# Placing VectorE's side work between two multiply-adds, and a strip of a gate on GpSimd

## The chip, the cores and the metric

One core of a Trainium2 chip. The metric is device time in microseconds (us), the median of the fast runs; executions of one kernel agree within about 0.2%. Five engines work side by side, each on its own list of instructions in order: TensorE (matrix products; PE, and PEld for its weight loads), VectorE (DVE), ScalarE (ACT), GpSimd (POOL) and SyncE (SP, which only starts transfers). They wait for one another through semaphores.

## The reference

Two parts, one after the other, for x of 8 x 3136 x 256 in float32:

```python
X = np.fft.fft(np.fft.fft(x, axis=1), axis=2).real          # mixing
h = np.maximum(X @ w_in, 0.0)                               # 256 -> 1024
conv = sum(conv_w[k] * shifted(h, k - 1) for k in range(3)) # along the sequence, per feature
out = (h * (1 / (1 + np.exp(-conv)))) @ w_out               # 1024 -> 256
```

## The kernel before

The transform along the sequence is done with products against DFT tables, after VectorE has *folded* the input (sums and differences of mirrored rows). The results of two half transforms are joined in *DFT sums* on VectorE. The transform along features is merged into `w_in`, as the matrix G. Then come 256 steps (8 batches x 4 chunks x 8 blocks of 128 features). In cycle t of the main loop, each engine works on several steps at once:

```python
for t in range(n + LAG):                      # LAG = 3
    sigmoid(steps[t - 2])                     # ScalarE, in two parts: GpSimd's columns, then VectorE's
    run("first")
    products(steps[t + 1])                    # TensorE: pb and pa, 386 to 418 columns
    copies(steps[t + 1])                      # ScalarE: pb from PSUM to SBUF, twice
    run("act")                                # ScalarE's copy for a DFT sum (u.copy)
    combine(steps[t])                         # VectorE, two instructions: h = relu(pa +- pb)
    run("dve")                                # VectorE: a fold, a DFT sum (u.fin) or a narrowing of weights
    seed(steps[t + 2])                        # ScalarE
    first_tap(steps[t])                       # ScalarE: g = w0 * h
    other_taps(steps[t - 1])                  # VectorE: g = w1 * h' + g, then g = w2 * h'' + g
    gate(steps[t - 2])                        # g = g * h, half on GpSimd and half on VectorE
    run("load")
    mm2(steps[t - LAG])                       # TensorE: the second product, po
    run("pe")                                 # TensorE: products pd of the next batch's DFT
```

(The guards at both ends of the loop are cut.) The side work for the next batch is spread over the cycles of this one. A DFT sum adds one half that ScalarE has copied out of PSUM and one that is still there:

```python
def copy(p):
    a_[sn, c] = asp.tile(...)
    nc.scalar.copy(out=a_[sn, c][:, 0:n], in_=p[:, 0:n])
def fin(p):
    a, bb, t = a_[sn, c], p[:, n:2 * n], PQ[b][sn]
    vt(t[:, 2 * c:Q4 + 1:4], a[:, 0:n], bb, op=ALU.add)
    vt(hi, x0, x1, op=ALU.subtract)
```

The last chunk of a batch is 832 columns wide; 64 of them make half an output tile, and are put into a tile `left` that two batches share.

## Time and profile before

| | before |
|---|---|
| median of fast runs | 1213.9 us |
| busy: TensorE, VectorE, ScalarE, GpSimd | 97%, 92%, 73%, 31% |
| VectorE waiting for ScalarE's copies at DFT sums | 56.3 us |
| steps whose second product starts late | 37 |
| time lost at these | 18.95 us |

"Late start" is used throughout for this: take the start-to-start time of neighbouring matrix instructions, subtract the 10th percentile of the same shape, and count a po run that begins over 0.05 us late after pa, together with the 0.105 us that its second instruction then loses as well.

### The profile page before, as it was taken

The numbers are of one execution on the slowest core, as the hardware profiler recorded it, in microseconds if no ns is written. First come the engines' busy times: TensorE is split into PE (matmuls) and PEld (weight loads), VectorE is DVE, ScalarE is ACT, GpSimd is POOL, SyncE is SP. The second block draws the span as 40 slices with busy tenths as digits, with TensorE's granted clock in tenths as the row PEclk, the third lists the DMA queues.
The fourth block names the chain that finished last, engine by engine and source line by source line (L and its number), as shares of the span: only waits on it lengthen the run. The fifth ranks groups of instructions, "written<-read, shape, count | busy, mean of one in ns | idle before, by whom it ended". The sixth has DMA issues, their size and how long they took to land.

```text
span 1214.1 us, 15439 instructions
## 1 busy us (share of the span) xinstructions
PE 1183.5 (97%) x4870; PEld 905.7 (75%) x4870; DVE 1120.7 (92%) x1689; ACT 880.5 (73%) x1837; POOL 373.5 (31%) x475
## 2 busy tenths in 40 slices
PE   5999999999999999999999999999999999999998
PEld 4676676777777777777777777777777777777776
DVE  7799999999999899998989999999998988899996
ACT  2477666777777777777777777777777777788884
POOL 5224534243233231424224242332222222222222
PEclk9999999999999999999999999999999999999999
DMA  9622233211131210302122020310001000110000
GB/s 222 195 12 86 83 37 103 64 53 42 39 89 49 66 41 14 93 26 73 33 75 63 1 80 27 94 40 26 27 1 53 31 26 27 46 34 27 26 27 31
DMA packets 70213, 66.30 MB, mean 55 GB/s; under 512 B 28123, under 2 KB 57827, under 8 KB 70131
## 3 DMA queue, kind: packets, MB, share of 16 engines
q1 hardware_dynamic: 64493, 52.18, 15.3%
q0 software_dynamic: 5120, 12.85, 3.7%
q8 instruction: 39, 0.64, 0.2%
q14 instruction: 43, 0.35, 0.1%
q10 hardware_dynamic: 518, 0.28, 0.1%
HBM read 39.53 MB, written 25.74 MB: 54 GB/s over the span
## 4 chain that ended last, share of the span: by engine, by line
PE 70%; DVE 21%; issue 4%; ACT 2%; DMA 0%; DVEq 0%; SPq 0%; ACTq 0%
PE po L94 43%; PE pb L94 10%; PE pa L94 10%; DVE g L725 7%; PE pd L94 6%; DVE h L713 3%; DVE g L746 3%; DVE xh L158 2%; ACT nb L702 1%; DVE xh L169 1%; DVE w L186 1%; DVE w L187 1%; ACT g L738 0%; DVE xh L173 0%; DVE pt L291 0%
## 5 line engine op out<-in xcount | busy, mean ns | idle before, releaser
L94 PE MATMUL po<-wout,g 128*128 128x256 f32 x3072 | 708.9, 380 | 9.8 <-DVE g L746 9.2
L94 PEld LDWEIGHTS po<-wout,g 128*128 128x128 f32 x3072 | 578.8, 190 | 162.6 <-DVE g L746 42.3
L725 DVE SCALAR_TENSOR_TENSOR g<-h,cw,g 128x770 f32<-128x770 f32 (+1 forms) x512 | 549.4, 1073 | 9.3 <-ACT g L719 0.2
L745 POOL TENSOR_TENSOR g<-g,h 128x385 f32<-128x385 f32 (+1 forms) x256 | 233.8, 913 | 762.0 <-ACT g L738 495.6
L738 ACT ACTIVATE g<-g 128x385 f32<-128x385 f32 (+2 forms) x512 | 244.1, 526 | 192.2 <-DVE g L725 191.7
L702 ACT ACTIVATE nb<-pb 128x386 f32<-128x386 f32 (+2 forms) x478 | 210.5, 493 | 86.4 <-PE pb L94 85.4
L713 DVE CUSTOM_DVE_ANT_0 h<-pa,nb 128x386 f32<-128x386 f32 (+2 forms) x495 | 257.0, 559 | 0.9 <-PE pa L94 0.9
L719 ACT ACTIVATE g<-h,cw 128x770 f32<-128x770 f32 (+1 forms) x256 | 243.2, 950 | 0.2 <-DVE h L713 0.2
L94 PE MATMUL pb<-qt,G 127*128 127x387 f32 (+2 forms) x512 | 212.7, 496 | 0.0
L94 PE MATMUL pa<-pt,G 128*128 128x387 f32 (+2 forms) x512 | 211.9, 494 | 0.0
L668 ACT ACTIVATE pa<-eb,ge 128x387 f32<-128x387 f32 (+2 forms) x252 | 151.4, 601 | 1.2 <-ACT ft L459 0.6
L94 PEld LDWEIGHTS pa<-pt,G 128*128 128x128 f32 x512 | 96.9, 189 | 73.6 <-issue 18.1
L746 DVE TENSOR_TENSOR g<-g,h 128x385 f32<-128x385 f32 (+1 forms) x256 | 146.2, 571 | 0.9 <-ACT g L738 0.9
L94 PE MATMUL pd<-tab,w 98*128 98x196 f32 (+3 forms) x448 | 126.7, 374 | 0.0
L133 POOL DMA_INDIRECT xh<-in_x_dram,idx x64 | 106.1, 1658 | 13.4 <-issue 9.2
L94 PEld LDWEIGHTS pb<-qt,G 127*128 127x128 f32 x512 | 93.9, 190 | 18.2 <-issue 0.9
L94 PEld LDWEIGHTS pd<-tab,w 98*128 98x128 f32 (+1 forms) x448 | 84.8, 191 | 12.3
L765 ACT COPY os<-po 128x256 f32<-128x256 f32 x196 | 57.4, 393 | 7.8 <-PE po L94 4.6
L158 DVE TENSOR_TENSOR xh<-xh 98x1020 f32<-98x1020 f32 (+1 forms) x32 | 40.7, 1277 | 2.7 <-DMA xh<-in_x_dram,idx 2.7
L169 DVE TENSOR_TENSOR xh<-xh 98x1024 f32<-98x1024 f32 (+1 forms) x32 | 41.3, 1291 | 0.1
L188 POOL COPY w<-xh 98x4 f32<-98x4 f32 (+1 forms) x32 | 19.6, 613 | 26.8 <-DVE xh L169 14.8
L291 DVE TENSOR_TENSOR qt<-as,pd 128x197 f32<-128x197 f32 (+1 forms) x14 | 7.2, 516 | 20.3 <-ACT as L287 20.3
(117 smaller groups left out, 386.2 us busy)
## 6 DMA issues: line engine op xcount, KB each, us to landing
out_dram<-os SPq DMA_DIRECT2D x192, 128.0 KB
xh<-in_x_dram SPq DMA_DIRECT2D x16, 784.0 KB
eb<-ed SPq DMA_DIRECT2D x16, 193.5 KB
tab<-dft_seq_dram SPq DMA_DIRECT2D x4, 589.5 KB
raw<-in_moe_w_in_dram SPq DMA_DIRECT2D x4, 512.0 KB
raw<-in_moe_w_out_dram SPq DMA_DIRECT2D x1, 2048.0 KB
eb<-ed SPq DMA_DIRECT2D x8, 209.0 KB
eb<-ed SPq DMA_DIRECT2D x8, 193.0 KB
```

The source lines that it names most:

```text
L94: nc.tensor.matmul(o, l, r, start=start, stop=stop, skip_group_check=True)
L133: nc.gpsimd.indirect_dma_start(out=xh[b, h][0:NP, 7 - m].rearrange("p q d -> p (q d)"), out_offset=None, in_=bass.AP(tensor=x.tensor, offs ...
L158: vt(a[:, :, :, 1:D], a[:, :, :, 1:D], r[:, :, :, D - 1:0:-1], op=ALU.add)
L668: act(pa[s][:, 0:n], eb[b, c], AF.Copy, scale=ge[:, f:f + 1])
L702: act(nb[s][:, i, cols], p[:, cols], AF.Copy, scale=-1.0 if i else 1.0)
L713: nc.vector._custom_dve(TENSOR_ADD_SAT, out=to, in0=a[:, cols], in1=c[:, i, cols], s0=BIG, s1=0.0)
L719: act(gs[s], hs[s][:, 0:n], AF.Copy, scale=cw[:, 0, s[2]:s[2] + 1])
L725: stt(out=g, in0=h[:, k:k + n], scalar=cw[:, k, f:f + 1], in1=g, op0=ALU.mult, op1=ALU.add)
L738: act(gs[s][:, c], gs[s][:, c], AF.Sigmoid)
L745: gt(g[:, p], g[:, p], h[:, p], op=ALU.mult)
L746: vt(g[:, v], g[:, v], h[:, v], op=ALU.mult)
L765: nc.scalar.copy(out=osb[:, j % 2], in_=pt[:, j % 2])
```

## The change

The intent: side work between the two multiply-adds, so that VectorE has work while ScalarE's copy for a DFT sum is on its way; and 64 small instructions off VectorE.

```diff
-    def other_taps(s):
+    def tap(s, k):
         g, h, f = gs[s], hs[s], s[2]
         n = g.shape[1]
-        for k in (1, 2):
-            stt(out=g, in0=h[:, k:k + n], scalar=cw[:, k, f:f + 1], in1=g, op0=ALU.mult, op1=ALU.add)
+        stt(out=g, in0=h[:, k:k + n], scalar=cw[:, k, f:f + 1], in1=g, op0=ALU.mult, op1=ALU.add)
...
         if r.start < r.stop:
-            vt(left[:, f, b % 2 * LEFT:(b % 2 + 1) * LEFT], g[:, r], h[:, r], op=ALU.mult)
+            gt(left[:, f, b % 2 * LEFT:(b % 2 + 1) * LEFT], g[:, r], h[:, r], op=ALU.mult)
...
             combine(steps[t])
-        run("dve")
         if t + 2 < n:
             seed(steps[t + 2])
         if t < n:
             first_tap(steps[t])
+
         if 0 <= t - 1 < n:
-            other_taps(steps[t - 1])
+            tap(steps[t - 1], 1)
+        run("dve")
+        if 0 <= t - 1 < n:
+            tap(steps[t - 1], 2)
         if 0 <= t - 2 < n:
             gate(steps[t - 2])
```

## The prediction

> **What bounds the kernel now.** I read the page first (busy shares, chain), then the waits, then the start times of single instructions on TensorE and VectorE.
>
> ```profile
> PE 1183.5 (97%) x4870; PEld 905.7 (75%) x4870; DVE 1120.7 (92%) x1689; ACT 880.5 (73%) x1837; POOL 373.5 (31%) x475
> ...
> PE 70%; DVE 21%; issue 4%; ACT 2%; DMA 0%; DVEq 0%; SPq 0%; ACTq 0%
> ```
>
> TensorE carries 70% of the chain and VectorE 21%; ScalarE and GpSimd have room. So this is a kernel on TensorE that sometimes hands the lead to VectorE. How much is lost at those places? The waits name them:
>
> ```profile
> PEld po L94 <- DVE g L746: 42.3, 74, 2.6
> PE po L94 <- DVE g L746: 9.2, 20, 1.9
> DVE qt L291 <- ACT as L287: 20.3, 14, 3.1
> DVE pt L291 <- ACT as L287: 19.4, 14, 3.3
> DVE as L310 <- ACT as L306: 16.6, 15, 3.2
> DVE wout L533 <- ACT wout L527: 4.4, 1, 4.4
> ```
>
> Columns: total in us, times, longest. Lines 1 and 2: the second product (po) waits for VectorE's half of the gate. The first is idle time of the weight load, which runs ahead of the products, so it is more than what is lost; the second is less, because the ends of products are modelled. Lines 3 to 5: 56.3 us in which VectorE sits at the head of a DFT sum until ScalarE's copy of the other half has landed.
>
> To size the loss I took start-to-start times of neighbouring matrix instructions and subtracted the 10th percentile of the same shape (a po instruction 0.215 us, a pair for pa or pb 0.65 us). From 44.5 us, where the steps begin, to the end the excess is 29.0 us. Of it 15.05 us stands before the first po instruction of 37 steps, with 3.9 us more before the second of those same 37 (0.105 us each). The other 10 us is scatter and changes of shape that VectorE has no part in. So 18.95 us is all that this change can give back in the steps: 1.6% of 1213.42 us. By time: 3.4 us before 150 us, 7.8 us from 150 to 310 us, 7.8 us after that. A late example, on VectorE and then TensorE:
>
> ```profile
> 421.09 1.02 DVE L713 CUSTOM_DVE_ANT_0 h<-pa,nb 128x386 f32<-128x386 f32 x2
> 423.68 0.52 DVE L291 TENSOR_TENSOR qt<-as,pd 128x196 f32<-128x196 f32 x1 [1.57 <-ACT as L287]
> 424.04 0.52 DVE L294 TENSOR_TENSOR qt<-pd,as 128x196 f32<-128x196 f32 x1
> 424.39 2.04 DVE L725 SCALAR_TENSOR_TENSOR g<-h,cw,g 128x770 f32<-128x770 f32 x2
> ```
> ```profile
> 431.54 2.86 PE L94 MATMUL po<-wout,g 128*128 128x256 f32 x12
> ...
> 436.25 2.86 PE L94 MATMUL po<-wout,g 128*128 128x256 f32 x12 [0.21 <-DVE g L746]
> ```
>
> VectorE idles 1.57 us, does two folds in the next two cycles, and TensorE then starts po late twice (2.86 us where an undisturbed run of 12 shows 2.75). Idle time at a DFT sum comes back as a TensorE stall two or three cycles later.
>
> **What the Trainium skill says.** (1) "Perfetto Trace Analysis", section "Tensor Engine Instruction (MATMUL, LD_WEIGHTS)": the end of a matmul in a profile is estimated. The trace agrees: 12 po instructions of 380 ns start 0.216 us apart; so I count by starts. (2) "SBUF — State Buffer", section "Who interferes with whom": VectorE with two SBUF inputs and GpSimd reading SBUF exclude each other, for a whole instruction. The trace agrees:
>
> ```profile
> 91.56 0.86 POOL L745 TENSOR_TENSOR g<-g,h 128x385 f32<-128x385 f32 x1 [4.96 <-ACT g L738]
> ```
> ```profile
> 91.78 2.52 DVE L725 SCALAR_TENSOR_TENSOR g<-h,cw,g 128x770 f32<-128x770 f32 x2
> ```
>
> The pair of multiply-adds that met GpSimd's gate took 2.52 us and not the usual 2.07. In most steps the combination (PSUM and one SBUF input, two of them, 1.0 us) lies over GpSimd's 0.86 us, and nothing collides. (3) "GPSIMD Engine Reference", section "3.1 Elementwise — side-by-side cycle accounting": about 2.6 cycles an element for a tensor_tensor. At the 1.2 GHz the page counts with that is 0.83 us for 385 columns; the trace has 913 ns mean. For 64 columns my estimate from it is 0.14 us plus some hundredths.
>
> **The change part by part.**
>
> *Order within a cycle.* Before: combine, side work (fold, DFT sum or narrowing), multiply-add 1, multiply-add 2, gate. After: combine, multiply-add 1, side work, multiply-add 2, gate. No instruction is added. The first multiply-add needs only the first tap of a step begun a cycle earlier, which is long there. It takes about 1.0 us (2.07 us a pair), so each wait at a DFT sum shrinks by up to 1.0 us. The three rows have 43 waits, 56.3 us, mean 1.31 us. Some are 3 us long, so I estimate 0.9 us recovered per wait, 39 us of VectorE time, leaving about 17 us. The narrowing's 4.4 us shrinks by 1.0 us, but at 62 us, where TensorE loses nothing.
>
> Behind a fold nothing is gained: its inputs are there in either order, and fold plus two multiply-adds take the same time.
>
> VectorE time is not span. After 310 us it has idle time in plenty; only the lead of up to 1 us that it carries into the following heavy cycles counts. In the example, the 1.0 us covers both late starts. In the stretch at 485 to 508 us the wait is 0.96 us and the late starts after it add up to 1.2 us. I estimate 65% of the 7.8 us, 5 us. From 150 to 310 us VectorE waits only 7.2 us in all (3.4, 2.8 and 1.0 in the three rows), against late starts of 7.8 us; perhaps 60% of those waits turns into TensorE time: 4 us. Before 150 us there are no DFT sums to wait at: 0.
>
> *The shared tile's columns.*
>
> ```profile
> L748 DVE TENSOR_TENSOR left<-g,h 128x64 f32<-128x64 f32 x64 | 14.0, 218 | 0.0
> ```
>
> 64 instructions of 218 ns, but the combination starts 0.14 us after each of them begins, so they hold VectorE 64 x 0.14 = 9 us, 8 of every 32 steps. On GpSimd each follows directly behind the 384-column gate, both fed by the same sigmoid. GpSimd starts that gate about 0.2 us after the combination starts and ends about 0.1 us after it. With the combination 0.14 us earlier and GpSimd about 0.15 to 0.2 us longer at the lock, the next multiply-add is held up by roughly 0.3 us, where 0.14 us was saved. Net I count 0.15 us lost in each such step. It matters only where VectorE leads: the last part of batch 0 and the late starts near 490 to 508 us and its like. That costs about 1 us of span. TensorE uses the shared tile as its seventh, 2.6 us into po, so it does not wait for it.
>
> Sum: 5 + 4 - 1 = 8 us, so 1213.4 - 8 = 1205 us.
>
> **The rivals.**
>
> *All of it comes back.* If every late start is covered by the lead, 19 us go: 1194.5 us. For: each late start after 310 us follows a wait. Against: those before 150 us follow none, and from 150 to 310 us VectorE is 96% busy (95.92 and 96.08 of 100 us in the two stretches from 100 to 300 us), so there is not enough idle time to reclaim.
>
> *The lock eats it.* GpSimd's extra instruction now stands against two-input multiply-adds in all 64 steps; if each costs 0.3 us more and VectorE leads in half of them, 10 us are lost and the result is 1214 to 1216 us. Against: VectorE has slack in most of those steps.
>
> *The DFT sum ends too late.* Its PSUM buffer is single, and the next unit's products (pd) start in the same cycle. Where VectorE does not wait, the sum now ends 1.0 us later. At 618 us the sum ended 1.0 us before pd began, with a wait of 1.59 us that the multiply-add fits into. So pd might be held by some tenths where VectorE is already behind: up to 2 us in all, 1207 us.
>
> *Nothing.* TensorE bound, VectorE's waits were slack: 1212 to 1214 us. The example at 421 us speaks against it.
>
> **Range and chances.** The ceiling of 19 us is 1.6%, so faster by over 2% would need something outside the steps; the start (first 44 us) and the tail (po back to back for the last 13 us) are not touched. Slower by 2% would need 24 us of new waits. I give 1198 to 1211 us for 8 in 10, chances 0.01 faster, 0.98 same, 0.01 slower.
>
> **What would show it.** Right: the three waits of VectorE for ScalarE's copies fall from 56 to below 25 us; po's late starts fall from 37 to some 15 to 20, those before 150 us staying; TensorE's other spacing unchanged; the shared tile's columns on GpSimd at about 0.2 us; multiply-adds after the combination in the 832-column steps a few tenths longer than their 1.1 us. Wrong: pd waiting for VectorE's DFT sums; GpSimd's short instruction taking 0.6 us or more; late starts as many as before although the 56 us have gone (then the lead is lost elsewhere); or a gain above 15 us, which would say that the early late starts also had their cause in the order.

## More of the kernel before

The groups of instructions that carry the argument. Columns: busy us and mean ns of one; then idle time of the engine before them and what ended it.

```profile
L725 DVE SCALAR_TENSOR_TENSOR g<-h,cw,g 128x770 f32<-128x770 f32 (+1 forms) x512 | 549.4, 1073 | 9.3 <-ACT g L719 0.2
L745 POOL TENSOR_TENSOR g<-g,h 128x385 f32<-128x385 f32 (+1 forms) x256 | 233.8, 913 | 762.0 <-ACT g L738 495.6
```

L725 are the two multiply-adds of each step, half of all of VectorE's time; L745 is GpSimd's half of the gate.

## The result, and the profile after

Ratios here are the mean time of one kernel's fast runs over that of the other's of the same rounds, so not quite the ratio of the medians that are quoted.

The changed kernel takes 1202.09 us (1201.56 to 1202.96) against 1213.91 us: ratio 0.9903, 95% interval 0.9886 to 0.992. That is 11.8 us less. The prediction was 1205 us, and 1198 to 1211 us as the range.

The first lines and the chain of the changed kernel's page:

```profile
PE 1175.7 (98%) x4870; PEld 907.1 (76%) x4870; DVE 1129.6 (94%) x1625; ACT 883.7 (74%) x1837; POOL 487.8 (41%) x539
...
PE 84%; DVE 10%; issue 1%; ACT 1%; DMA 0%; ACTq 0%; DVEq 0%; SPq 0%
```

TensorE's share of the chain went from 70 to 84%, VectorE's from 21 to 10%. VectorE lost 64 instructions and is nevertheless 9 us *busier*, and GpSimd is 114 us busier. Its multiply-adds, and GpSimd's half of the gate:

```profile
L724 DVE SCALAR_TENSOR_TENSOR g<-h,cw,g 128x770 f32<-128x770 f32 (+1 forms) x512 | 579.9, 1133 | 6.0 <-ACT g L719 2.2
L744 POOL TENSOR_TENSOR g<-g,h 128x385 f32<-128x385 f32 (+1 forms) x256 | 270.5, 1058 | 626.0 <-ACT g L737 429.3
```

Most of this is time that the two spend waiting for each other inside an instruction, as is shown below for one step. The new work on GpSimd itself is small: I estimate 19 us (64 instructions of the 0.29 us that one takes undisturbed). The changed kernel's waits (total us, times, longest):

```profile
DVE pt L291 <- ACT as L287: 13.3, 13, 2.1
DVE qt L291 <- ACT as L287: 12.6, 13, 2.1
PEld po L94 <- DVE g L745: 12.5, 17, 1.6
...
DVE as L310 <- ACT as L306: 8.4, 9, 2.5
```

VectorE's waits at DFT sums went from 56.3 to 34.3 us, and TensorE's weight load now waits 12.5 us for the gate where it was 42.3 us. (All lines below L725 have moved up by one in this kernel: the gate on VectorE is L745, on GpSimd L744, the shared tile L747, the multiply-adds L724.) The same cycle of batch 2 as in the prediction's example, VectorE and then TensorE in order of time:

```profile
412.56 1.02 DVE L713 CUSTOM_DVE_ANT_0 h<-pa,nb 128x386 f32<-128x386 f32 x2
413.50 1.21 DVE L724 SCALAR_TENSOR_TENSOR g<-h,cw,g 128x770 f32<-128x770 f32 x1
415.68 0.51 DVE L291 TENSOR_TENSOR qt<-as,pd 128x196 f32<-128x196 f32 x1 [0.97 <-ACT as L287]
```
```profile
423.48 2.75 PE L94 MATMUL po<-wout,g 128*128 128x256 f32 x12
427.71 2.75 PE L94 MATMUL po<-wout,g 128*128 128x256 f32 x12
```

A multiply-add now lies in what was idle time, and the po runs that were 2.86 us long and began late are 2.75 us long and follow at once. VectorE still waits 0.97 us here. It had waited 1.57 us, and the multiply-add took more than the difference: VectorE now comes to this point earlier, because it is ahead.

Late starts, number and us, worked out alike for every kernel. VectorE's waits are the sum of its rows for ScalarE's copies at DFT sums.

| kernel | median us | ratio to before | VectorE's waits | up to 150 us | 150 to 310 us | after 310 us |
|---|---|---|---|---|---|---|
| before | 1213.91 | 1 | 56.3 | 4, 3.39 | 11, 7.79 | 22, 7.77 |
| changed | 1202.09 | 0.9903 | 34.3 | 3, 2.39 | 7, 3.51 | 2, 0.86 |
| e1_order_only | 1202.23 | 0.9906 | 35.9 | 3, 2.37 | 7, 4.36 | 0 |
| e2_left_only | 1215.55 | 1.0015 | 55.8 | 5, 4.26 | 11, 7.09 | 23, 8.89 |
| e3_sums_only | 1203.23 | 0.9911 | 30.5 | 4, 3.46 | 5, 3.26 | 0 |
| e4_folds_only | 1209.14 | 0.9958 | 57.7 | 3, 2.37 | 8, 6.02 | 14, 4.70 |
| e5_copy_early | 1202.96 | 0.9908 | 19.2 | 4, 3.49 | 5, 3.14 | 0 |
| e6_order_copy_early | 1201.49 | 0.9896 | 9.3 | 3, 2.36 | 5, 3.09 | 0 |
| e7_sums_last | 1203.89 | 0.9918 | 6.7 | 4, 3.52 | 5, 3.50 | 0 |
| e8_skew | 1206.31 | 0.9934 | 8.8 | 6, 3.05 | 6, 4.89 | 0 |
| e9_gathers | 1199.99 | 0.9878 | 9.8 | 2, 0.87 | 5, 3.08 | 0 |
| e10_folds_late | 1198.48 | 0.9869 | 9.4 | 2, 0.88 | 4, 2.22 | 0 |
| e11_after_again | 1202.31 | 0.9900 | 35.2 | 3, 1.96 | 7, 3.50 | 2, 0.84 |

From before to changed the late starts shrink by 18.95 - 6.76 = 12.2 us, and the median time by 11.8 us. The two executions that were profiled lie further apart, 14.3 us in span (1214.1 and 1199.8 us). Of this 1.6 us is the start: the steps begin at 44.5 and 43.0 us, which the change can't have caused, since they begin at 44.1 us in the second profile of the changed kernel. That leaves 0.5 us for everything else, so nearly all of the gain is found in the late starts. All runs gave correct results.

### The profile page after: what moved, and what is told of

It reads as the page before. It is cut to its first block, busy times and chain, and to the rows that moved or that the text cites. A ratio compares the mean times of both kernels' runs of the same rounds, so it can differ in the third digit from the quotient of the medians.

```text
span 1199.8 us, 15442 instructions
## 1 busy us (share of the span) xinstructions
PE 1175.7 (98%) x4870; PEld 907.1 (76%) x4870; DVE 1129.6 (94%) x1625; ACT 883.7 (74%) x1837; POOL 487.8 (41%) x539
## 4 chain that ended last, share of the span: by engine, by line
PE 84%; DVE 10%; issue 1%; ACT 1%; DMA 0%; ACTq 0%; DVEq 0%; SPq 0%
PE po L94 51%; PE pb L94 12%; PE pa L94 12%; PE pd L94 8%; DVE g L724 5%; DVE h L713 1%; DVE g L745 1%; DVE xh L158 0%; DVE xh L169 0%; ACT nb L702 0%; DVE w L187 0%; DVE raw L540 0%; DVE wout L533 0%; ACT g L737 0%; ACT os L764 0%
## 5 line engine op out<-in xcount | busy, mean ns | idle before, releaser
L724 DVE SCALAR_TENSOR_TENSOR g<-h,cw,g 128x770 f32<-128x770 f32 (+1 forms) x512 | 579.9, 1133 | 6.0 <-ACT g L719 2.2
L744 POOL TENSOR_TENSOR g<-g,h 128x385 f32<-128x385 f32 (+1 forms) x256 | 270.5, 1058 | 626.0 <-ACT g L737 429.3
L745 DVE TENSOR_TENSOR g<-g,h 128x385 f32<-128x385 f32 (+1 forms) x256 | 146.6, 572 | 2.1 <-ACT g L737 2.1
L747 POOL TENSOR_TENSOR left<-g,h 128x64 f32<-128x64 f32 x64 | 65.6, 1025 | 0.0
L764 ACT COPY os<-po 128x256 f32<-128x256 f32 x196 | 57.7, 392 | 7.9 <-PE po L94 4.7
L188 POOL COPY w<-xh 98x4 f32<-98x4 f32 (+1 forms) x32 | 34.8, 1088 | 39.0 <-DVE xh L169 28.4
```

The costliest lines, as they stand in the source:

```text
L724: stt(out=g, in0=h[:, k:k + n], scalar=cw[:, k, f:f + 1], in1=g, op0=ALU.mult, op1=ALU.add)
L744: gt(g[:, p], g[:, p], h[:, p], op=ALU.mult)
L745: vt(g[:, v], g[:, v], h[:, v], op=ALU.mult)
L747: gt(left[:, f, b % 2 * LEFT:(b % 2 + 1) * LEFT], g[:, r], h[:, r], op=ALU.mult)
L764: nc.scalar.copy(out=osb[:, j % 2], in_=pt[:, j % 2])
```

## The experiments

All were timed in five rounds beside the kernel before, and their 95% intervals are about 0.0015 wide to each side (1.8 us). e5 to e8 were timed together on another chip than the rest, and e9 to e11 later than e1 to e4; across these groups, differences of 1 or 2 us are within the noise. Theories: **A**, the waits at DFT sums are filled, and that is all; **B**, taking 64 instructions off VectorE matters; **C**, the place of the folds matters too. D to F come later.

### The two halves of the change

e1_order_only is the changed kernel with the shared tile's columns back on VectorE:

```diff
-            gt(left[:, f, b % 2 * LEFT:(b % 2 + 1) * LEFT], g[:, r], h[:, r], op=ALU.mult)
+            vt(left[:, f, b % 2 * LEFT:(b % 2 + 1) * LEFT], g[:, r], h[:, r], op=ALU.mult)
```

> The new order between the two multiply-adds, with the shared tile's columns left on VectorE. Theory A (the gain is VectorE's waits at the DFT sums being filled by a multiply-add; the move to GpSimd is neutral or a slight loss): as fast as the changed kernel's 1202 us or up to 3 us faster, 1199 to 1203 us, ratio to the kernel before 0.987 to 0.991, VectorE's waits for ScalarE's copies 30 to 38 us (56 before, 34 in the changed kernel). Theory B (the relief of VectorE by 64 instructions carries a good part of the gain): 1206 to 1210 us, ratio 0.994 to 0.997.

Measured 1202.23 us, ratio 0.9906 (0.9891 to 0.9921): the same as the changed kernel. e2_left_only is the kernel before with the opposite edit (`vt` to `gt` in that line, nothing else):

> The old order, with the shared tile's columns on GpSimd. Theory A: 1213 to 1216 us, ratio 0.999 to 1.002; VectorE's waits for ScalarE's copies stay near 56 us, and the short GpSimd instruction averages over 0.7 us because it waits behind VectorE's two-input instructions. Theory B: 1206 to 1210 us, ratio 0.994 to 0.997.

Measured 1215.55 us, ratio 1.0015 (1.0002 to 1.0029): 1 to 2 us *slower* by the medians (0.2 to 3.5 us by the interval). So B falls, and all of the gain that can be measured is the order. The instruction on GpSimd, in the changed kernel:

```profile
L747 POOL TENSOR_TENSOR left<-g,h 128x64 f32<-128x64 f32 x64 | 65.6, 1025 | 0.0
```

It takes 1.03 us on average, and not the 0.2 us of the prediction. Why is seen in one step, VectorE's line and then GpSimd's two:

```profile
471.31 1.11 DVE L724 SCALAR_TENSOR_TENSOR g<-h,cw,g 128x832 f32<-128x832 f32 x1
```
```profile
470.67 0.87 POOL L744 TENSOR_TENSOR g<-g,h 128x384 f32<-128x384 f32 x1 [3.25 <-issue]
471.49 1.09 POOL L747 TENSOR_TENSOR left<-g,h 128x64 f32<-128x64 f32 x1
```

GpSimd's gate ends at 471.54; VectorE's multiply-add, which has begun at 471.31, gets the shared access first and keeps it until 472.42, and the 64 columns are done right after, at 472.58. Where VectorE was not in the way the same instruction took 0.29 us. It waits inside the instruction, so the time counts as busy.

### Which side work matters

e3_sums_only puts only the DFT sums between the multiply-adds (they get a place "fin" of their own), e4_folds_only only the folds and the narrowing. Both have the shared tile's columns on VectorE.

```diff
 # both
-            at(cs[i + 1], "dve", u.fin)
+            at(cs[i + 1], "fin", u.fin)
 # e3_sums_only                     # e4_folds_only
         combine(steps[t])                  combine(steps[t])
+        run("dve")                 +       run("fin")
         ...                                ...
         tap(steps[t - 1], 1)               tap(steps[t - 1], 1)
+        run("fin")                 +       run("dve")
         tap(steps[t - 1], 2)               tap(steps[t - 1], 2)
```

> Only the DFT sums stand between the two multiply-adds; folds and narrowing stay in front of both; the shared tile's columns on VectorE. Theory A: all of the gain of the order, so within 1.5 us of e1_order_only, 1199 to 1204 us. Theory C (the place of the folds matters too, because what meets GpSimd's gate on the shared SBUF access changes): half of the gain or less, 1206 us or more.

> Only folds and narrowing stand between the two multiply-adds; the DFT sums stay behind the combination as before; the shared tile's columns on VectorE. Theory A: no gain, 1211 to 1215 us, ratio 0.998 to 1.001, VectorE's waits for ScalarE's copies stay over 50 us. Theory C: a gain of 4 us or more, 1209 us or less.

Measured: 1203.23 us for the sums alone, as A says, and 1209.14 us for the folds alone, ratio 0.9958 (0.9945 to 0.9972). That is 4.7 us off, so A is not the whole story: C has found something that the waits don't show. VectorE's waits at DFT sums stay at 57.7 us in this kernel, and late starts after 310 us still shrink from 7.77 to 4.70 us. One cycle with a fold of batch 2, first before and then in e4_folds_only:

```profile
426.82 1.02 DVE L713 CUSTOM_DVE_ANT_0 h<-pa,nb 128x386 f32<-128x386 f32 x2
427.76 1.27 DVE L158 TENSOR_TENSOR xh<-xh 99x1020 f32<-99x1020 f32 x1
428.95 2.07 DVE L725 SCALAR_TENSOR_TENSOR g<-h,cw,g 128x770 f32<-128x770 f32 x2
430.93 0.55 DVE L746 TENSOR_TENSOR g<-g,h 128x385 f32<-128x385 f32 x1
431.40 0.55 DVE L713 CUSTOM_DVE_ANT_0 h<-pa,nb 128x386 f32<-128x386 f32 x1
```
```profile
422.63 1.02 DVE L713 CUSTOM_DVE_ANT_0 h<-pa,nb 128x386 f32<-128x386 f32 x2
423.57 1.01 DVE L724 SCALAR_TENSOR_TENSOR g<-h,cw,g 128x770 f32<-128x770 f32 x1
424.50 1.21 DVE L158 TENSOR_TENSOR xh<-xh 99x1020 f32<-99x1020 f32 x1
425.63 1.01 DVE L724 SCALAR_TENSOR_TENSOR g<-h,cw,g 128x770 f32<-128x770 f32 x1
426.56 0.55 DVE L745 TENSOR_TENSOR g<-g,h 128x385 f32<-128x385 f32 x1
```

From the combination's start to the next one's it was 431.40 - 426.82 = 4.58 us; with the same instructions in the other order it is 427.03 - 422.63 = 4.40 us (the next combination starts at 427.03). Start to start, two things differ:

- *The multiply-adds.* Back to back, where the second reads and writes what the first has just written, the second starts 1.05 us after the first (median of the 770-column steps): the first runs for 1.01 us, and then VectorE is idle for 0.036 us, in all 256 steps. Other instructions start before the one in front has ended: with a fold in between, the fold starts 0.93 us after the first multiply-add. That is 0.12 us a cycle. (The expectation of e8_skew below says 1.01 us and 0.08 us; it left out the idle time.)
- *What follows the combination.* GpSimd's gate often still runs 0.2 us into that instruction. In the kernel before, a fold of 1020 columns directly behind the combination takes 1.13 us from start to start when GpSimd has under 0.1 us to go, 1.19 us at 0.15 to 0.2 us and 1.24 us at 0.2 to 0.25 us. A multiply-add in that place lasts 1.01 us up to 0.2 us of overlap and 1.05 us at 0.2 to 0.25 us; beyond, it lengthens with the overlap, to 1.24 us at 0.4 and 1.53 us at 0.7 us. So a multiply-add is the better neighbour by 0.05 to 0.07 us. In the cycle shown it is 0.06 us (the fold takes 1.19 us, then 1.13 us).

Together they make up the 0.18 us. Over the cycles with a fold, without a DFT sum and with 770-column steps, from 150 to 1150 us (60 before, 59 in e4_folds_only), the median time from one combination to the next falls from 4.64 to 4.47 us and the mean from 4.67 to 4.60 us. This adds up over the folds of seven batches, and the list of waits shows nothing there. How much of the 4.7 us of kernel time each of the two brings was not separated.

### Taking the waits away at the root

If A is right, the same gain must come without touching VectorE's order, by making ScalarE's copy earlier. e5_copy_early is the kernel before with one word changed; e6_order_copy_early is e1_order_only with the same edit.

```diff
-            at(cs[i + 1], "act", u.copy)
+            at(cs[i + 1], "first", u.copy)
```

> The kernel before, its order on VectorE untouched, but ScalarE makes the copy that a DFT sum waits for ahead of its copies of the next step's products and not behind them. Theory A: this takes away the same waits at their root, so VectorE's waits for ScalarE's copies fall from 56 to under 10 us, the late starts of the second product after 310 us fall from 22 to under 6, and the time is 1201 to 1205 us. Rival: the waits were slack, or the earlier copy holds up ScalarE's other copies by its 0.33 us; then 1211 us or more.

> e1_order_only with ScalarE's copy for the DFT sums early as well. Theory A: e1_order_only has no late start after 310 us any more, so taking away its last 36 us of waits can only act between 150 and 310 us: 1200 to 1202 us, at most 2 us faster than e1_order_only. If the waits were worth something in themselves it would be 1198 us or less.

e5_copy_early: 1202.96 us, ratio 0.9908 (0.9892 to 0.9923), with no late start after 310 us. The waits that are left, 19.2 us, are more than I expected: once ahead, VectorE also comes before the early copy. They cost nothing that can be seen after 310 us. e6_order_copy_early: 1201.49 us, 0.7 us less than e1_order_only (within the noise), with 9.3 us of waits against 35.9. So the 34 us that the changed kernel still waits are slack. A is confirmed twice: waits filled or waits removed give the same time, and more than enough of either gives nothing further.

### A sum that ends later

e7_sums_last is e3_sums_only with the sums behind both multiply-adds:

```diff
-        run("fin")
         tap(steps[t - 1], 2)
+        run("fin")
         gate(steps[t - 2])
```

> e3_sums_only, but the DFT sums stand behind both multiply-adds, right in front of the gate. Theory A alone: the waits for ScalarE's copies shrink further, to under 15 us, and the time stays at 1202 to 1204 us. Theory D (a DFT sum that ends later holds the next unit's products, because the sum's PSUM buffer is single): the products pd now start late behind VectorE's sums and the time is 1206 us or more.

1203.89 us: between the two. The waits shrink to 6.7 us and bring nothing. Theory D is right in kind and small: products pd that start late after po cost 1.8 us between 150 and 310 us (0.2 us in the kernel before, 0.7 us in e3_sums_only), and nothing after 310 us. Its threshold of 1206 us was not reached.

### Keeping the multiply-adds apart in all steps

e8_skew starts from e6_order_copy_early and does the second multiply-add of a step one cycle later, so that its neighbour is one of another step.

```diff
-    LAG = 3
+    LAG = 4
-            tap(steps[t - 1], 2)
-            gate(steps[t - 2])      # and sigmoid(steps[t - 2])
+            tap(steps[t - 2], 2)
+            gate(steps[t - 3])      # and sigmoid(steps[t - 3])
-    hp: bufs=4    asp: bufs=4    osp: bufs=3, tiles of two outputs
+    hp: bufs=5    asp: bufs=3    osp: bufs=5, tiles of one output
```

> e6_order_copy_early with the second multiply-add of a step one cycle later, so that it no longer follows the first one of the same step, and the gate and second product a cycle later too (one more buffer for h, single-tile output buffers to make room for it). Theory E (two multiply-adds of one step back to back cost VectorE 0.08 us more than with another instruction between them: 1.01 against 0.93 us from start to start; this is why e4_folds_only gained 4.7 us): start to start falls to 0.93 to 0.95 us in all 256 steps, some 20 us of VectorE's time, and most of the 6.7 us of late starts left before 310 us go: 1196 to 1199 us. Rival F (e4's gain was only that the multiply-add meets the end of GpSimd's gate in place of the fold): the spacing stays at 1.01 us and the time within 1 us of e6_order_copy_early.

The mechanism holds: neighbouring multiply-adds of 770 columns are now 0.93 to 0.94 us apart (25th percentile and median of 76), where those of one step were 1.05 us apart. So it is the dependence that costs the 0.12 us, and F falls as the only cause; the fold's 0.06 us stays. The time does not follow: 1206.31 us, 4.8 us slower than e6_order_copy_early. Its scatter and late starts from 44.5 us on add up to 19.4 us against 14.7 us, all of the difference before 310 us: the first steps wait at pa and pb (1.7 us more), and VectorE now waits 21.6 us for the sigmoid. Which of the longer lag, the buffers and the sigmoid is to blame was not separated and stays open. After 310 us there was nothing left to gain, since e6_order_copy_early already had no late start there: VectorE's saved time was worth nothing.

### What is left, and a faster version

The largest late start of the changed kernel is at 113 us, 1.2 us, in a stretch without DFT sums. GpSimd in front of it, then VectorE:

```profile
98.64 1.51 POOL L133 DMA_INDIRECT xh<-in_x_dram,idx  x1 [0.19 <-issue]
100.46 2.20 POOL L133 DMA_INDIRECT xh<-in_x_dram,idx  x1 [0.30 <-PE po L94]
102.96 3.69 POOL L133 DMA_INDIRECT xh<-in_x_dram,idx  x1 [0.30 <-ACT g L737]
...
106.86 1.69 POOL L744 TENSOR_TENSOR g<-g,h 128x385 f32<-128x385 f32 x2
```
```profile
106.20 3.18 DVE L724 SCALAR_TENSOR_TENSOR g<-h,cw,g 128x770 f32<-128x770 f32 x1
```

Three indirect gathers hold up GpSimd's queue; then two gates, of two steps, run in one go, and VectorE's multiply-add takes 3.18 us where it should take 1.0. It ends 0.83 us after the second gate (109.38 and 108.55), but it had begun 0.66 us before the first, while the last gather still ran. What held it in that time stays open. Two edits on e6_order_copy_early follow; e10_folds_late has both.

```diff
 # e9_gathers: one gather a cycle
-        at(NF + 1 + j // 3, "load", fn)
+        at(NF + 1 + max(j - 1, 0), "load", fn)
 # e10_folds_late: folds of batch 2 over 20 cycles, not 16
-    ends = [9, 20, per + 4] + ...
+    ends = [9, 20, per + 8] + ...
```

> e6_order_copy_early with the four indirect gathers of the second half of batch 1 one in each of four cycles, where three stand in one cycle now. Theory A (the late starts before 150 us do not come from VectorE's waits at DFT sums but, the largest of them at 113 us in the changed kernel, from GpSimd, which runs three gathers in front of a gate while VectorE's multiply-add waits for it): the late start of 1.2 us near 113 us goes, the time falls by 0.5 to 1.5 us against e6_order_copy_early, 1200 to 1201 us. Rival: VectorE is too full there in any case, and the late start only moves: no change.

> e9_gathers with the folds of batch 2 spread over 20 cycles where they had 16. If VectorE is simply too full between 150 and 245 us (8 DFT sums and 14 folds at once), the 3 us of late starts that are left there in e6_order_copy_early go in part: 1197.5 to 1200 us, and this is then the fastest version. Rival: the work only moves to where batch 2's sums stand: 1200 to 1202 us.

> The changed kernel again, beside these. 1201.5 to 1202.5 us, ratio 0.989 to 0.991.

e9_gathers: 1199.99 us; the late start at 113 us is gone, those up to 150 us shrink from 2.36 to 0.87 us, and the median time by 1.5 us against e6_order_copy_early, which was timed in other rounds. e10_folds_late: 1198.48 us (1198.06 to 1199.09), ratio 0.9869 (0.9853 to 0.9886). Its edit does one thing more than its name says: batch 2's DFT starts when its folds end, so its products and sums begin four cycles later, over 21 cycles in place of 25, and the folds of batch 3 move and crowd in the same way. Which of these brings the 1.5 us against e9_gathers was not separated. In the same rounds the changed kernel took 1202.31 us (1201.61 to 1202.88). So e10_folds_late is the fastest version here, 3.8 us below the changed kernel and 16 us below the kernel before, with 3.1 us of late starts left.

## Why the prediction was right or wrong

The time, 1202.09 us, lies in the range and 2.9 us below the value; the class (within 2%) was right as well. Step by step:

- **The bound and the ceiling held.** Late starts shrank by 12.2 us and the median time by 11.8 us. No experiment, not even the fastest, saved more than the 18.95 us.
- **The mechanism held.** It is shown by e3_sums_only (sums alone, nearly the full gain) and independently by e5_copy_early (the waits removed instead of filled).
- **The size after 310 us was too small.** "I estimate 65% of the 7.8 us, 5 us": measured 7.77 - 0.86 = 6.9 us, and 7.8 us in e1_order_only. In the worst stretch I set one wait of 0.96 us against 1.2 us of late starts, as if no lead could be carried in from earlier waits. e3_sums_only has no late start after 310 us, so the sums alone were enough for all of them. From 150 to 310 us it was 4.3 us, as predicted (4). Up to 150 us it was 1.0 us, where I had 0.
- **"Behind a fold nothing is gained" was wrong.** It rested on "its inputs are there in either order, and fold plus two multiply-adds take the same time". They do not: 4.40 against 4.58 us in one cycle, and 4.7 us of kernel time in e4_folds_only. 2.07 us for a pair hid it, but the profile before could have told: the 9.3 us of idle time in its line for L725 are 256 gaps of 0.036 us, and in its trace the second multiply-add starts 1.05 us after the first while the gate starts 0.94 us after the second. This also explains the gain up to 150 us, which e4_folds_only shows in the same size (3.39 to 2.37 us). The two gains overlap: 10.6 us for the sums, 4.7 us for the folds, 11.6 us for both, because either one can remove the same late start.
- **The waits left over were mis-sized.** "I estimate 0.9 us recovered per wait, 39 us": it was 22 us, and 34.3 us are left where I said 17. An engine that gets ahead arrives earlier at the next wait. e6_order_copy_early shows that these waits are slack.
- **The shared tile's columns were mis-sized, in a term that hardly counted.** About 0.2 us was predicted for the GpSimd instruction, with VectorE held up by it; 1.03 us was measured, because it is mostly GpSimd that waits for VectorE's multiply-add. The net cost of about 1 us of span was of the right size in the old order (1 to 2 us, e2_left_only); in the new order it is too small to be seen (e1_order_only).
- **Its own signs were mixed.** Of those for "right", the waits were to fall below 25 us (34.3 us measured), and the late starts to 15 to 20, with the early ones staying (12 measured, 3 of the 4 early ones left). Of those for "wrong", one came: GpSimd's short instruction takes over 0.6 us. It speaks against the small term on the shared tile alone, since the late starts carry the gain.
- **The rivals.** "The lock eats it" can be seen in busy time (VectorE's multiply-adds 1133 ns each against 1073) and not in the time of the kernel, since VectorE has room for it where TensorE leads. "The DFT sum ends too late" is real and small, as e7_sums_last shows.

## What to carry to other kernels

When the bound engine starts late behind a second engine, look for that engine's idle time some cycles earlier, put independent work into it, or make what it waits for earlier; either does, and what is left of the waits afterwards may be slack. Size such a gain by the bound engine's late starts and not by the waits or by busy time, which can rise while the kernel gets faster. The order of instructions on one engine has a price of its own: two that depend on each other back to back, or the wrong neighbour for another engine's access to memory, cost up to 0.12 us a cycle here, and the list of waits shows nothing of it. Compare start-to-start times, not durations, to find it.

## What the Trainium skill lacked or had wrong

- "VectorE: DVE Perf Modes", section "The DRAIN you can't avoid", says that in its measurement chaining VectorE's instructions with or without semaphores made no difference. It gives no cost for a neighbour that depends on the instruction in front. Here two multiply-adds on the same tile are 1.05 us apart from start to start, and 0.93 us with an independent instruction between them or with one of another step behind (e8_skew).
- "SBUF — State Buffer", section "Who interferes with whom": the page calls the ports that VectorE and GpSimd share an exclusive lock, and this is borne out (64 columns on GpSimd took 1.03 us on average, and 0.29 us where VectorE was not in the way). It does not say that a short remainder is free: by the recorded ends, a multiply-add directly behind the combination loses nothing while GpSimd has under 0.2 us to go, and a fold begins to lose somewhere between 0.1 and 0.2 us.
- The same section infers that a tensor_tensor on VectorE leaves GpSimd's writing of descriptors alone. No run here settles it: in the changed kernel one indirect gather that lay beside instructions of VectorE with two SBUF inputs all the time took 0.97 us (at 11.9 us), and another nearly all the time beside such took 3.69 us (at 103 us).
- "GPSIMD Engine Reference", section "3.1 Elementwise — side-by-side cycle accounting": its 2.6 cycles an element gave an estimate of 0.14 us for 64 columns. The page names the dispatch and the joining of the cores as further terms, without a figure for GpSimd. The shortest gate of 384 columns took 0.86 us and the shortest strip of 64 took 0.29 us in the changed kernel; from these two I estimate 1.8 ns a column and a fixed 0.18 us.
